# Moving the first group's casts off VectorE and reordering the start of the second group in a fused attention and routing kernel

## The chip, the cores and the metric

The kernel runs on one core of a Trainium2 chip (trn2). The metric is the device time of one execution in microseconds (us), as a median over executions. Executions of both kernels were timed in turn on the same chip, and one execution of each kernel was profiled.

Two words are used throughout. A **unit** is one head by 128 keys: TensorE (PE) makes 128x768 scores, ScalarE (ACT) takes their exp, PE multiplies with the values. **Exp n** is the exp of unit n, counted from 0; 24 units make a group (one batch, four heads), and there are eight groups. A **half-clock window** is a stretch of 3.41 us in which the granted TensorE clock, as the trace records it, is 0.50 (in the profile of the kernel before: from 43.86 to 47.28 us). In the profile lines DVE is VectorE, POOL is GpSimd and SPq is SyncE's queue.

## The reference, cut to what matters

```python
# q, k, v: (4, 8, 768, 64); proj: (64, 6)
q_bits = (q @ proj > 0); k_bits = (k @ proj > 0)      # 6 hash bits a row
mask   = bucket(q_bits)[:, :, :, None] == bucket(k_bits)[:, :, None, :]
attn   = softmax(where(mask, q @ k.T / 8, -1e9))
x      = (attn @ v) as (3072, 512)
# then: P = exp(x @ w_gate), 8 rounds of row and column scaling,
#       out = sum over 8 experts of P[:, e] * relu(x @ w1[e]) @ w2[e]
```

## The kernel before

Each group has to be prepared. VectorE turns q and k in 32x32 blocks (`turn_qk`), PE hashes them, VectorE makes bits, and the 71-row operands `ks` and `qs` of the score matmuls are put together from 64 rows of q or k and 7 rows of bits. From the second group on, GpSimd casts the turned rows to f16, transfers issued by SyncE stack the heads (`stack`), and the bits travel to DRAM and back (`put_bits`, `get_bits`). The first group does all of it with engine copies (`place`), as there is nothing else to do yet.

```python
def turn_qk(name, c):
    ...
    pin(nc.vector.transpose(o_ap, i_ap))
    if n:
        pin(nc.gpsimd.tensor_copy(t16s[name][:, c, :], trs[name][:, c, :]))

def at_once():                       # group 0
    for name in "kq":
        for c in range(2):
            turn_qk(name, c)
            place(name, 0, c, nc.scalar.copy)
            ...                      # the hash matmuls
            warm_up((0, 1, 0, 6)[2 * (name == "q") + c])
    for i, name in enumerate("kq"):
        ...                          # bits of k, then of q, on VectorE
        place_bits(name, 0)
        for c in range(2):
            if name == "k":
                place("k", 1, c, nc.scalar.copy)
                place("q", 1, c, nc.vector.tensor_copy)
    cast_v()
    for h in range(1, HG):
        for name in "kq":
            if h > 1:
                for c in range(2):
                    place(name, h, c, nc.vector.tensor_copy)
            place_bits(name, h)
...
# groups 1 to 7: at which unit of the group before each step is issued
due = (5, 6, 7, 8, 15, 17) if n == 1 else (0, lag, 2 * lag, 3 * lag, 4 + 3 * lag, 7 + 3 * lag)
...                                  # k turned, stacked
if n + 1 < len(groups):
    fetch(n + 1, "k")
...                                  # q turned, stacked, v loaded; hash, bits, put_bits
if n + 1 < len(groups):
    fetch(n + 1, "q")
...                                  # get_bits, the other heads stacked, cast_v
```

The units themselves run in a fixed order on PE, ACT and VectorE, each engine in program order. A product of two SBUF operands on VectorE, `xn`, ends each head:

```python
pin(nc.vector.tensor_tensor(xns[b][:, :, c0:c0 + D], nv[:, :, 0:D],
                            rn.unsqueeze(2).to_broadcast([P, J, D]), op=Alu.mult))
```

Near the end of attention GpSimd makes eight additions of 128x1024 f16 on the weights of expert 1 (`quarters_of_w(1)`, `quarters_of_w2(1)`).

The softmax here doesn't subtract the row's maximum and nothing guards it: scores larger than these inputs give would overflow.

Of the kernel before, what the change touches and what calls it, by code (L numbers as in the profile page):

```python
# [20 lines left out]
def kernel(  # L21
# [11 lines left out]
    nc = tc.nc  # L33
# [17 lines left out]
    HG = 4  # L51
# [10 lines left out]
    def pin(ins):  # L62
        tc.keep_in_program_order(ins)
        return ins
# [281 lines left out]
    groups = [(b, g) for b in range(B) for g in range(NGRP)]  # L346
    nat, grp = {}, {}

    def fetch(n, what, eng=nc.gpsimd):
        b, g = groups[n]  # L350
        for name, src in (("k", k), ("q", q)):
            if name in what:
                x = (12 if n else 0) + 3 * "kq".index(name)
                t = acc_flat[:, x * DD:(x + 3) * DD].rearrange("p (m d) -> p m d", d=D)
                pin(eng.dma_start(out=t, in_=src[b, g * HG:(g + 1) * HG].rearrange("h (r m) d -> (h r) m d", r=R)))
                nat[name, n] = t
        if "v" in what:
            t = lv.tile([P, HG, KT * D], F32, tag="v", name="v")
            vsrc = v[b, g * HG:(g + 1) * HG].rearrange("h (r m j) d -> m r h (j d)", r=R, m=M4)
            for m in range(M4):  # L360
                pin(eng.dma_start(out=t[R * m:R * (m + 1)], in_=vsrc[m]))
            nat["v", n] = t

    def prepare(n):
# [3 lines left out]
        trs, bts, dss, t16s = {}, {}, {}, {}  # L368
        for x, name in enumerate("kq"):
            y = (18 if n else 6) + 3 * x  # L370
            trs[name] = acc_flat[:, y * DD:(y + 3) * DD].rearrange("p (c t) -> p c t", c=2)
            d[name] = wk.tile([P, HG, S], F16, tag=name + "s", name=name + "s")
            if n == 2:
                if x == 0:
                    t16 = hpool.tile([P, FO, S], F16, tag="h", name="t16")
                t16s[name] = t16[:, 2 * x:2 * x + 2, :]
            elif n:
                t16s[name] = wk.tile([P, 2, S], F16, tag="t16", name="t16")

        def turn_qk(name, c):  # L380
            i_ap = nat[name, n][:, :, 32 * c:32 * (c + 1)]
            o_ap = trs[name][:, c, :]
            if name == "k":
                i_ap = i_ap.rearrange("p (m t) d -> p m t d", m=M4)
                o_ap = o_ap.rearrange("p (t m r) -> p m t r", t=KT, m=M4)
            else:
                o_ap = o_ap.rearrange("p (m r) -> p m r", r=R)
            pin(nc.vector.transpose(o_ap, i_ap))
            if n:
                pin(nc.gpsimd.tensor_copy(t16s[name][:, c, :], trs[name][:, c, :]))  # L390

        def stack(name, h):
            for c in range(2):
                pin(nc.sync.dma_start(out=d[name][32 * c:32 * (c + 1), h, :],
                                         in_=t16s[name][32 * h:32 * (h + 1), c, :]))
# [22 lines left out]
        def get_bits(name, h):  # L418
            pin(nc.sync.dma_start(out=d[name][D:KR, h, :].rearrange("r (j t) -> r j t", j=2),
                                       in_=dss["kq"]["kq".index(name), :, h, 0:NB + 1, :].rearrange("j r t -> r j t")))  # L420
# [6 lines left out]
        def cast_v():  # L427
            v32 = wk.tile([P, 2, 3, D], F32, tag="v32", name="v32", bufs=1)
            for i in range(2):
                hs = slice(2 * i, 2 * i + 2)  # L430
                pin(nc.gpsimd.tensor_copy(va[:, hs, :, 0:D],
                                          nat["v", n][:, hs, :].rearrange("p h (t d) -> p h t d", d=D)))
            for i in range(2):
                hs = slice(2 * i, 2 * i + 2)
                pin(nc.gpsimd.tensor_tensor(v32, va[:, hs, 0:3, 0:D], va[:, hs, 3:6, 0:D], op=Alu.add))
                pin(nc.gpsimd.tensor_tensor(v32[:, :, 0], v32[:, :, 0], v32[:, :, 1], op=Alu.add))
                pin(nc.gpsimd.tensor_tensor(vs[:, hs, 0:D], v32[:, :, 0], v32[:, :, 2], op=Alu.add))

        def place(name, h, c, copy):
            pin(copy(d[name][32 * c:32 * (c + 1), h, :], trs[name][32 * h:32 * (h + 1), c, :]))  # L440

        def place_bits(name, h):
            o, i = d[name][D:KR, h, :], d["bt"][32 * h:32 * h + NB + 1, "kq".index(name), :]
            if name == "k":
                pin(nc.vector.tensor_scalar(o, i, BIG, None, op0=Alu.mult))
            else:
                pin(nc.vector.tensor_copy(o, i))

        def at_once():
            d["bt"] = wk.tile([P, 2, S], F16, tag="t16", name="bt0")  # L450
            for name in "kq":
                pr = sps.tile([P, 2, 512], F32, tag="s", name="pr0")
                d["pr" + name] = pr
# [3 lines that stand above are left out]
                    for x in range(2):  # L457
                        pin(nc.tensor.matmul(pr[:, x, 0:HT], pb0[:, c, :], trs[name][:, c, x * HT:(x + 1) * HT],
                                             start=(c == 0), stop=(c == 1)))
                    warm_up((0, 1, 0, 6)[2 * (name == "q") + c])  # L460
            for i, name in enumerate("kq"):
                pin(nc.vector.tensor_scalar(d["bt"][:, i, :].rearrange("p (x t) -> p x t", x=2),
                                            d["pr" + name][:, :, 0:HT], 0.0, qoff[:, 0:1] if i else 0.5,
                                            op0=Alu.is_gt, op1=Alu.subtract))
                place_bits(name, 0)
                for c in range(2):
                    if name == "k":
                        place("k", 1, c, nc.scalar.copy)
                        place("q", 1, c, nc.vector.tensor_copy)
            cast_v()  # L470
            for h in range(1, HG):
                for name in "kq":
                    if h > 1:
                        for c in range(2):
                            place(name, h, c, nc.vector.tensor_copy)
                    place_bits(name, h)

        if n == 0:
            at_once()
            return  # L480

        lag = 2 if n > 2 else 1
        due = (5, 6, 7, 8, 15, 17) if n == 1 else (0, lag, 2 * lag, 3 * lag, 4 + 3 * lag, 7 + 3 * lag)
        yield due[0]
        turn_qk("k", 0)
        yield due[1]
        turn_qk("k", 1)
        stack("k", 0)
        stack("k", 1)
        if n + 1 < len(groups):  # L490
            fetch(n + 1, "k")
        yield due[2]
        turn_qk("q", 0)
# [22 lines left out]
            move_bits("q")  # L516
        put_bits()
        stack("k", 2)
        if n + 1 < len(groups):
            fetch(n + 1, "q")  # L520
        yield due[5]
        for h in range(1 if n < 3 else 0, 2):
# [6 lines left out]
        stack("q", 3)  # L529
        get_bits("k", 3)  # L530
        get_bits("q", 3)
        cast_v()

    def scores(n, h, kt):
# [104 lines left out]
    def warm_up(count):  # L639
        for _ in range(count):  # L640
            pin(nc.tensor.matmul(warm, tiny, tiny.unsqueeze(1).to_broadcast([P, 4, P]), start=True, stop=True))

    warm_up(18)
    for _ in prepare(0):
        pass
# [8 lines left out]
    due = 0  # L654
    owed = 0.0
    for u in range(len(units) + 1):
        if u < len(units):
            n, h, kt = units[u]
            b, g = groups[n]
            i = u % per  # L660
            if i == 0:
                prep = prepare(n + 1) if n + 1 < len(groups) else iter(())
                due = 0
            while due is not None and due <= i:
                due = next(prep, None)
            if n == len(groups) - 1 and i == 2:
                for _ in quarters_of_w(1):
                    pass
                for _ in quarters_of_w2(1):
                    pass  # L670
            if u + 1 < len(units):
                pts[u + 1] = scores(*units[u + 1])
# [11 lines left out]
        elif u >= 2 * per:  # L684
            owed += (total if b < 3 else total - 8 * 865) / (2 * per - 8)
            while owed > 0:
                c = next(fill, None)
# [201 lines left out]
```

## Time and profile before

| | before |
|---|---|
| median | 779.89 us (779.07 to 780.59, 3 runs) |
| profiled execution, span | 776.6 us, mean granted clock 0.996 |
| PE busy | 752.2 us, 97% |
| VectorE / ACT / GpSimd busy | 73% / 66% / 40% |
| first exp starts | 16.46 us |
| exp 33 starts | 48.83 us |

The busy shares are averages over the whole span and say that PE sets the time. The change touches the first 66 us only, so what counts is the timeline of that stretch. In a timeline each line is one instruction or several merged ones: start, length, engine, source line, operation, output and inputs with their shapes, count, and in brackets the time its engine sat idle before it with what ended that. The lines are shown in the prediction below.

### The profile page before, as it was taken

Reading aid. Unit: us, or ns where it says so; the run is one execution under the profiler, and the core shown is the slowest. Engines: PE = TensorE matmul, PEld = TensorE weight load, DVE = VectorE, ACT = ScalarE, POOL = GpSimd, SP = SyncE. Lnnn points to the kernel's source line nnn. Section 1 sums busy time; section 2 is a strip of 40 time slices with the busy share of each in tenths; the row PEclk is TensorE's granted clock in tenths of the full one; section 3 lists DMA queues with packets and bytes.
Section 4 is the critical chain, followed back from the end, with each engine's and each line's share of the span. In section 5 each row is a group of like instructions: output and inputs, shape, how many; then the busy total and the mean of one; then the engine's idle time right before and its main releaser. Section 6 shows DMA issues by size and latency. Waiting matters only on the chain.

```text
span 776.6 us, 16594 instructions
## 1 busy us (share of the span) xinstructions
PE 752.2 (97%) x6245; PEld 518.6 (67%) x6245; DVE 570.3 (73%) x1265; ACT 512.6 (66%) x1026; POOL 309.9 (40%) x313
## 2 busy tenths in 40 slices
PE   8889999999999999999999999999999999999996
PEld 3556656566554666677777777777777777777663
DVE  6867757766669677777777777777777777777774
ACT  4877776678754777766666666666666666666660
POOL 5476535357400333443344334334543344334220
PEclk9999999999999999999999999999999999999999
DMA  6679548652011464586477647754964496443334
GB/s 203 142 180 208 159 115 210 141 141 55 2 35 22 79 109 81 107 143 110 83 124 132 119 90 136 119 100 82 171 121 90 84 162 109 82 93 75 83 83 132
DMA packets 40925, 87.55 MB, mean 113 GB/s; under 512 B 7028, under 2 KB 21196, under 8 KB 40844
## 3 DMA queue, kind: packets, MB, share of 16 engines
q0 software_dynamic: 27152, 69.49, 46.7%
q1 hardware_dynamic: 13020, 16.21, 8.0%
q8 instruction: 49, 0.80, 0.4%
q10 hardware_dynamic: 672, 0.79, 0.4%
q14 instruction: 32, 0.26, 0.1%
HBM read 53.01 MB, written 6.98 MB: 77 GB/s over the span
## 4 chain that ended last, share of the span: by engine, by line
PE 82%; DVE 7%; ACT 6%; DMA 2%; issue 2%; SPq 0%; ACTq 0%; DVEq 0%
PE a L767 18%; PE a L245 17%; PE d L767 13%; PE y L245 9%; PE st L538 5%; PE d L245 4%; PE hp L600 4%; ACT pt L541 4%; PE yp L610 3%; PE num L554 3%; PE hp L318 1%; PE pr L400 1%; PE yp L302 1%; ACT acc L236 1%; DVE hT L776 1%
## 5 line engine op out<-in xcount | busy, mean ns | idle before, releaser
L776 DVE CUSTOM_DVE_ANT_0 hT<-d,u 128x384 f16<-128x384 f32 x336 | 185.7, 553 | 96.0 <-ACT u L772 95.2
L249 ACT ACTIVATE vt<-a,p 128x256 f32<-128x256 f32 x324 | 153.2, 473 | 149.2 <-PE a L245 148.8
L541 ACT ACTIVATE pt<-st 128x768 f16<-128x768 f32 x192 | 146.5, 809 | 49.3 <-PE st L538 48.8
L772 ACT COPY u<-a 128x384 f32<-128x384 f32 x336 | 160.8, 479 | 23.0 <-PE a L767 20.6
L284 POOL DMA_DIRECT2D acc<-vt x72 | 61.3, 852 | 267.6 <-ACT vt L249 114.1
L245 PEld LDWEIGHTS <-hT 128*128 128x128 f16 x1296 | 126.3, 97 | 50.8 <-DVE hT L776 1.1
L245 PE MATMUL a<-t,hs 128*128 128x256 f16 x972 | 145.8, 273 | 2.1 <-ACT vt L249 1.0
L245 PEld LDWEIGHTS <-hs 128*128 128x128 f16 x972 | 94.8, 98 | 38.5 <-issue 2.8
L767 PEld LDWEIGHTS <-t 128*128 128x128 f16 x896 | 87.7, 98 | 36.1 <-issue 0.3
L767 PE MATMUL a<-xT,s 128*128 128x384 f16 x448 | 109.4, 326 | 0.2
L767 PE MATMUL d<-xd,t 128*128 128x384 f16 x448 | 109.4, 326 | 0.0
L538 PE MATMUL st<-qs,ks 71*128 71x384 f16 x384 | 94.2, 327 | 7.1 <-ACT pt L541 2.7
L245 PE MATMUL y<-t,hT 128*128 128x256 f16 x648 | 97.1, 272 | 0.0
L253 DVE SCALAR_TENSOR_TENSOR acc<-y,p,acc 128x256 f32<-128x256 f32 x162 | 77.5, 479 | 11.4 <-PE y L245 11.4
L554 PEld LDWEIGHTS <-pt 128*128 128x128 f16 x1152 | 60.8, 98 | 27.4 <-issue 1.4
L767 PEld LDWEIGHTS <-s 128*128 128x128 f16 x672 | 65.5, 98 | 17.5 <-issue 2.6
L554 PE MATMUL num<-va,pt 128*128 128x65 f16 x1152 | 66.8, 194 | 1.3 <-DVE nv L565 0.7
L806 ACT ACTIVATE hT<-a 128x384 f16<-128x384 f32 x112 | 54.0, 483 | 1.8 <-PE a L767 1.7
L767 PE MATMUL a<-xd,s 128*128 128x384 f16 x224 | 54.3, 323 | 0.8 <-ACT u L772 0.6
L767 PE MATMUL d<-xT,t 128*128 128x384 f16 x224 | 54.7, 326 | 0.0
L767 PE MATMUL a<-xT,t 128*128 128x384 f16 x224 | 54.7, 326 | 0.0
L538 PEld LDWEIGHTS <-ks 71*128 71x128 f16 x384 | 33.5, 98 | 31.5 <-issue 16.2
(116 smaller groups left out, 987.4 us busy)
## 6 DMA issues: line engine op xcount, KB each, us to landing
acc<-vt POOLq DMA_DIRECT2D x72, 512.0 KB, 4.8
t<-in_moe_w_dram POOLq DMA_DIRECT2D x24, 512.0 KB, 7.7
v<-in_v_dram POOLq DMA_DIRECT2D x28, 192.0 KB, 6.0
out_dram<-acc SPq DMA_DIRECT2D x82, 64.0 KB
acc<-in_k_dram POOLq DMA_DIRECT2D x6, 768.0 KB, 5.9
acc<-in_q_dram POOLq DMA_DIRECT2D x6, 768.0 KB, 13.2
t<-in_moe_w_dram POOLq DMA_DIRECT2D x4, 1024.0 KB, 12.4
ks<-t SPq DMA_DIRECT2D x56, 48.0 KB
```

What stands on the lines that cost most here:

```text
L245: pin(nc.tensor.matmul(dst, hq[hn][:, fo, :], wq[wn][:, fo, :], start=first and fo == 0, stop=fo == FH - 1, skip_group_check=True))
L249: pin(nc.scalar.activation(out=vt[:, k], in_=a, func=Act.Copy, scale=p))
L253: pin(nc.vector.scalar_tensor_tensor(out=dst, in0=src, scalar=p, in1=dst, op0=Alu.mult, op1=Alu.add))
L284: pin(nc.gpsimd.dma_start(out=acc[:, b, i], in_=vt, accum_op=Alu.add))
L538: pin(nc.tensor.matmul(st[:, i, 0:HT], d["k"][0:KR, h, kt * P:(kt + 1) * P], d["q"][0:KR, h, i * HT:(i + 1) * HT], start=True, stop=True))
L541: pin(nc.scalar.activation(out=pt, in_=st[:, :, 0:HT], func=Act.Exp, scale=scale))
L554: pin(nc.tensor.matmul(num[:, j * (D + 1):(j + 1) * (D + 1)], pf[:, j * P:(j + 1) * P], va[:, h, kt, :], start=(kt == 0 and j == 0), stop= ...
L600: pin(nc.tensor.matmul(hp[:, 0:HT], w1[:, do, fo * P:(fo + 1) * P], xT[:, do, b * S + t * HT:b * S + (t + 1) * HT], start=(do == 0), stop= ...
L767: pin(nc.tensor.matmul(bk, wq[wn][:, do, f * P:(f + 1) * P], xq[xn][:, do, :], start=first and do == 0, stop=do == 1, skip_group_check=True))
L772: pin(nc.scalar.copy(t, bk))
L776: pin(add(TENSOR_ADD_SAT, out=dst, in0=bk, in1=u, s0=3e38, s1=0.0))
L806: pin(nc.scalar.activation(out=hT[:, f, hi], in_=a, func=Act.Relu))
```

## The change

Its intent is to relieve VectorE in the opening, and to get the bits of the second group on their way sooner. The first group's late heads (k heads 2 and 3, q heads 1 to 3) are cast by GpSimd in whole tiles and stacked by ten SyncE transfers. The second group is turned at units 3 to 6 and hashed at 9, and the third group's loads move behind its bits in program order.

```diff
-            if n == 2:
+            if n in (0, 2):
                 ...                  # room for the f16 copies of group 0
-            if n:
-                pin(nc.gpsimd.tensor_copy(t16s[name][:, c, :], trs[name][:, c, :]))
+            pin(nc.gpsimd.tensor_copy(t16s[name][:, c, :], trs[name][:, c, :]))
...
-                    warm_up((0, 1, 0, 6)[2 * (name == "q") + c])
+                    warm_up(6 if name == "q" and c else 0)
+                for h in range(2 if name == "k" else 1, HG):
+                    stack(name, h)
...
-                for c in range(2):
-                    if name == "k":
-                        place("k", 1, c, nc.scalar.copy)
-                        place("q", 1, c, nc.vector.tensor_copy)
+            for c in range(2):
+                place("k", 1, c, nc.scalar.copy)
             cast_v()
             for h in range(1, HG):
                 for name in "kq":
-                    if h > 1:
-                        for c in range(2):
-                            place(name, h, c, nc.vector.tensor_copy)
                     place_bits(name, h)
...
-        due = (5, 6, 7, 8, 15, 17) if n == 1 else (...)
+        due = (3, 4, 5, 6, 9, 12) if n == 1 else (...)
...
-        if n + 1 < len(groups):      # twice: for k and for q
+        if n > 1 and n + 1 < len(groups):
...
+        if n == 1:
+            fetch(2, "kq")           # after get_bits
         cast_v()
```

More of the change, by code (lines that the diff above doesn't have):

```diff
@@ L376, in prepare @@
                 t16s[name] = t16[:, 2 * x:2 * x + 2, :]
-            elif n:
+            else:
                 t16s[name] = wk.tile([P, 2, S], F16, tag="t16", name="t16")
@@ L482, in prepare @@
         lag = 2 if n > 2 else 1
-        due = (5, 6, 7, 8, 15, 17) if n == 1 else (0, lag, 2 * lag, 3 * lag, 4 + 3 * lag, 7 + 3 * lag)
+        due = (3, 4, 5, 6, 9, 12) if n == 1 else (0, lag, 2 * lag, 3 * lag, 4 + 3 * lag, 7 + 3 * lag)
         yield due[0]
@@ L518, in prepare @@
         stack("k", 2)
-        if n + 1 < len(groups):
+        if n > 1 and n + 1 < len(groups):
             fetch(n + 1, "q")
```

## The prediction

> **What bounds the kernel now.** I read the page first (engine shares, slices, chain), then the windows of the first 66 us, then the timelines of PE, ACT, DVE, GpSimd and of the SyncE queue over the same stretch, and last the chain of waits from 6 to 50 us. The page and the windows:
>
> ```profile
> PE 752.2 (97%) x6245; PEld 518.6 (67%) x6245; DVE 570.3 (73%) x1265; ACT 512.6 (66%) x1026; POOL 309.9 (40%) x313
> ...
> PE 82%; DVE 7%; ACT 6%; DMA 2%; issue 2%; SPq 0%; ACTq 0%; DVEq 0%
> ...
> 42.00:50.00 8.00, 6.46 (x59) 3.08 (x60) 5.60 (x11) 4.04 (x6) 7.84 (x13) 0.79 0.56 170
> 50.00:66.00 16.00, 14.65 (x205) 10.32 (x203) 10.30 (x21) 15.85 (x23) 9.22 (x15) 1.00 0.88 206
> ```
>
> The whole kernel hangs on TensorE. The shares of DVE, ACT and DMA in the chain lie mostly in the first 66 us, where the first of eight groups (a batch and four of its heads; a group is 24 units, one head by 128 keys each) get going: group 0 must be turned, hashed and scored before anything else exists to do. The change touches only this opening. In the good stretch (50 to 66) ACT is busy 15.85 of 16 us: there the exp of each unit is the limit. From 42 to 50 ACT is busy only half the time and the mean granted clock is 0.79: something is lost there. The exps of line 541 show what (start, length, engine, idle before, releaser):
>
> ```profile
> 23.65 3.69 ACT L541 ACTIVATE pt<-st 128x768 f16<-128x768 f32 x5
> 27.91 0.81 ACT L541 ACTIVATE pt<-st 128x768 f16<-128x768 f32 x1 [0.57 <-PE st L538]
> 30.22 0.81 ACT L541 ACTIVATE pt<-st 128x768 f16<-128x768 f32 x1 [1.50 <-PE st L538]
> 32.83 1.51 ACT L541 ACTIVATE pt<-st 128x768 f16<-128x768 f32 x2 [1.80 <-PE st L538]
> ...
> 43.86 1.59 ACT L541 ACTIVATE pt<-st 128x768 f16<-128x768 f32 x2 [1.39 <-PE st L538]
> 47.38 0.81 ACT L541 ACTIVATE pt<-st 128x768 f16<-128x768 f32 x1 [1.93 <-PE st L538]
> 48.83 1.51 ACT L541 ACTIVATE pt<-st 128x768 f16<-128x768 f32 x2 [0.64 <-PE st L538]
> ```
>
> The reader is to see two holes, 27 to 33 and 42 to 49 us. The steady pace is the first fifteen exps in 10.88 us, 0.725 us a unit. The first exp starts at 16.46, so unit 17 should start at 16.46 + 17 x 0.725 = 28.79; it starts at 32.83: **4.04 us lost**. Exps 0 to 29 are done at 42.4, so exp 33 should start three paces later, at 44.6; counting two exps from 43.86 and one at 47.38, it is the one at 48.83: **4.2 us lost**. What they wait for is in the chain:
>
> ```profile
> 28.72 0.94 DVE acc L388
> ...
> 30.36 0.60 DVE xn L570
> 30.97 0.05 issue
> 31.01 0.51 PE xp L576 x6
> 31.52 0.83 PE pr L400 x8
> ...
> 34.26 6.99 DMA ds<-bt
> ...
> 41.60 1.54 DMA qs<-ds
> ```
>
> In the first hole VectorE is late: its queue still holds group 0's casts when group 1's transposes, the division of the heads and the turn of x come due. In the second, the bits of group 1 travel to DRAM in 6.99 us and back in 1.54 us, behind 768 KB of v and 768 KB of the third group's q; PE stands 1.53 us before the scores of unit 30. Right after it the window 43.9 to 47.2 shows a granted clock of 0.50, for one stretch of about 3.4 us, the only one after the start.
>
> [...] one window at 0.50 follows a window (40.4 to 43.8) in which PE was busy 1.87 of 3.40 us. [...] the placing of k bits (7x768 f16) takes 0.35 us while GpSimd rests and 0.86 us at 15.87 us, when GpSimd holds a 0.92 us addition; the f32 transposes take 0.90 to 0.98 us with or without GpSimd. [...] SyncE's loads, which land in the order of their issue, the last (q of group 1) at 17.0 us.
>
> **The change, part by part.**
>
> (1) Start. VectorE now does this between k's bits and the first score:
>
> ```profile
> 12.66 0.35 DVE L445 TENSOR_SCALAR ks<-bt 7x768 f16<-7x768 f16 x1
> 13.04 1.11 DVE L440 CAST qs<-acc 32x768 f16<-32x768 f32 x2
> 14.19 1.02 DVE L462 TENSOR_SCALAR bt<-pr,qoff 128x768 f16<-128x768 f32 x1
> 15.24 0.60 DVE L447 COPY qs<-bt 7x768 f16<-7x768 f16 x1
> ```
>
> The two casts in between (1.11 us) go. The q bits then wait for the q hash, which ends on PE at 10.88 + 2.83 = 13.71, not for the casts at 14.15. So they start about 0.45 us sooner, and their placing at about 14.75 meets the end of GpSimd's first v cast (14.03 to 14.83) rather than the middle of the second: 0 to 0.25 us more[...]. First score at about 15.4 instead of 15.94: **0.5 us saved**. The single warm-up matmul that goes sat beside this wait, worth nothing.
>
> (2) Late heads. Ten casts of 32x768 go from VectorE: the pair of part (1), 1.11 us, and four more pairs in its timeline up to 24 us, 1.80 + 1.26 + 1.12 + 1.12 us. Together 6.41 us leave VectorE before 24.3. In their place GpSimd makes four 128x768 casts (0.83 us each, 3.3 us, at 8 to 12.6 us, where it idled 8.55 us for v), and SyncE issues ten transfers of 48 KB at 0.57 us each, from about 8.8 to 15.6. These are off the path if they land in time. They queue behind group 1's loads, which end at 17.0; 480 KB at the 220 GB/s that the 1536-byte v rows showed is 2.2 us, so the last lands near 19.3 and the third pair (q head 1) near 18.3. Unit 6 wants q head 1 at 15.4 + 6 x 0.725 = 19.8. It fits by about 1.5 us.
>
> (3) First hole. With VectorE free some 6 us sooner (its bits placed at about 18 to 19.5 us instead of 24.3), group 1's four transposes (3.8 us) run at units 3 to 6 and are done by about 23, in time for the hash at units 9 and 10 (22.4 to 23.8). The hash itself stays: sixteen matmuls are one 1.43 us piece in every later group. So is a turn of x, which the second stretch shows at about 0.15 us net. Lost then: 1.43 + 0.15, call it 1.6 with the split, instead of 4.04: **2.4 us saved**. The hash no longer falls on the unit of the turn of x.
>
> (4) Second hole. The bits of group 1 leave at about 25 instead of 34.3 us. Even with another 7 us on the way and 2 us back they are there at 34; unit 30 comes at 15.9 + 30 x 0.725 + 1.6 = 39.3. The 1.53 us wait goes, and with PE no longer idle so does the half-clock window. Lost then: only group 2's hash, about 1.4 us, instead of 4.2: **2.8 us saved**.
>
> (5) Third group's loads. They leave GpSimd after v of group 1 and the gate weights, near 26 to 27 us; before, k left at 27.0 and q at 33.5. They land by about 33, and group 2 is turned from unit 24, near 35. Nothing on the path. Nothing else in the program changes.
>
> Sum: 0.5 + 2.4 + 2.8 = 5.7 us. From 66 us on PE is busy 131.5 of 134 us and then 563 of 576, with waits that move along with it, so the gain should go through to the end. I take off 0.5 us for a short wait at unit 9 or 10, where the transposes end close to the hash. 779.9 - 5.2 = **774.7 us**.
>
> **The rivals.** A: the stacked heads come late. Ten small transfers sit behind 1.5 MB on the same queue. For it: the margin at unit 6 is estimated, and the DMA engines are full until 17 us, as the DMA view of 0 to 24 us shows (40 slices of 0.6 us):
>
> ```profile
> DMA  0000192899999999999999899992000000000000
> ```
>
> Against it: this queue goes empty at 17 us and stays so until 26. A wait of 2 us plus a half-clock window would eat about 3 us and leave 777.5. B: GpSimd becomes the bound of the opening, as it also converts v (14.0 to 20.0 us) and now starts group 1's casts right behind. [...] Against it: those casts are needed only by unit 24. Worst, part (3) gives 1 us less: 775.7. C: the bits' round trip still ends late, since all of the third group's 1.5 MB now meets it instead of half: the 7 us could become some 13, an estimate from the same rate. Then unit 30 waits as before and only (1) and (3) remain: 777. Against it: nine microseconds of lead. D: the half-clock window comes back elsewhere[...]; about 1.5 us: 776.2. E: all goes a little better, as no wait is left at the hash and the exps close ranks: 773.5.
>
> **Range and chances.** The parts are worth 5.2, and A, B, C, D each take at most 3 us and are not all likely at once; the runs of the kernel before lie within 1.5 us. So 772.8 to 777.6 holds it 8 times in 10. 2% is 15.6 us, more than all the idle time in the opening could give: faster 0.005, within 0.985, slower 0.01 (only a new long wait or more half-clock windows would do that).
>
> **What would show it.** First exp at about 16.0 instead of 16.46. No casts of 32x768 on VectorE at 13 to 24 us. Exp 17 at about 29.9 instead of 32.8 and exp 33 near 43 (15.97 + 33 x 0.725 + 3.0) instead of 48.8. No wait for a bits transfer in the PE timeline at 40 to 44 us and the granted clock 1.00 throughout. Wrong would be a PE wait on a transfer into ks or qs near 19 to 21 us, or a clock of 0.50 in the opening, or a gain in the first 66 us that the span doesn't show.

The 0 to 0.25 us in part (1) is an estimate, the 0.60 us of placing q's bits beside a GpSimd cast of v less the 0.35 us of k's bits without one. That the half-clock window goes with the wait (part 4) was an estimate from the one window of this trace, and so was its 1.5 us in rival D. The transposes took 0.93 to 0.98 us. The last of each of SyncE's loads landed at 6.93 (k), 9.80 (q), 10.63 to 13.88 (four of v), 15.41 and 17.27 us (k and q of group 1).

## The result

| | before | after |
|---|---|---|
| median | 779.48 us (779.01 to 780.59, 4 runs) | 774.41 us (773.42 to 776.04, 4 runs) |
| ratio | | 0.9935, 95% interval 0.9912 to 0.9958 |
| profiled execution, span | 776.6 us | 771.7 us |

A ratio is the mean time of one kernel's fast runs over that of the other's of the same rounds, so it is not quite the ratio of the medians. The time came out at 774.4 us against 774.7 predicted: faster, by less than 2%.

Now the profile after. On its page the chain that ended last gives DVE and DMA a smaller share and ACT a larger one; the windows view (stretch; busy time of PE, PEld, DVE, ACT and GpSimd with counts; granted clock; DMA share; GB/s) shows the full clock where 0.79 stood:

```profile
PE 83%; ACT 8%; DVE 6%; issue 2%; DMA 1%; SPq 0%; ACTq 0%; DVEq 0%
...
42.00:50.00 8.00, 7.32 (x98) 5.09 (x95) 4.30 (x11) 7.38 (x12) 2.12 (x4) 1.00 1.06 233
```

The exps of the profile after, in the timeline of ACT:

```profile
15.09 7.29 ACT L539 ACTIVATE pt<-st 128x768 f16<-128x768 f32 x10 [1.52 <-PE st L536]
22.97 0.81 ACT L539 ACTIVATE pt<-st 128x768 f16<-128x768 f32 x1 [0.59 <-PE st L536]
24.37 4.40 ACT L539 ACTIVATE pt<-st 128x768 f16<-128x768 f32 x6 [0.59 <-PE st L536]
29.33 11.02 ACT L539 ACTIVATE pt<-st 128x768 f16<-128x768 f32 x15 [0.57 <-PE st L536]
41.27 0.81 ACT L539 ACTIVATE pt<-st 128x768 f16<-128x768 f32 x1 [0.92 <-PE st L536]
42.67 16.90 ACT L539 ACTIVATE pt<-st 128x768 f16<-128x768 f32 x23 [0.59 <-PE st L536]
```

Counting 10 + 1 + 6 exps puts exp 17 at 29.33, and 15 + 1 more put exp 33 at 42.67. Both holes are gone but for short gaps of 0.57 to 0.92 us: two at a hash of group 1, one at the turn of x, two at a hash of group 2. VectorE's timeline after, between k's bits and the first score, has no casts:

```profile
11.94 0.35 DVE L444 TENSOR_SCALAR ks<-bt 7x768 f16<-7x768 f16 x1
13.02 1.02 DVE L463 TENSOR_SCALAR bt<-pr,qoff 128x768 f16<-128x768 f32 x1 [0.73 <-PE pr L457]
14.08 0.39 DVE L446 COPY qs<-bt 7x768 f16<-7x768 f16 x1
```

q's bits wait for their hash (0.73 us), as foreseen. And SyncE's queue shows the bits of group 1 leaving at 25.77 and the transfer back issued at 30.28 (it waits for their arrival in DRAM). In the chain before they arrived at 34.26 + 6.99 = 41.25, so this is 11.0 us sooner:

```profile
25.77 0.53 SPq L415 DMA_DIRECT2D ds<-bt  x1
...
30.28 0.30 SPq L418 DMA_DIRECT2D ks<-ds  x1
```

**Where the gain goes later.** I laid the 1026 ACT instructions of the two profiles side by side and took the lead of the new kernel at each. It is 1.37 us at exp 0, 3.50 at exp 17, 6.16 at exp 33, then constant at 6.2 to 6.4 until 186 us (times of before); between 186 and 200 us it falls to 4.53, and it is 4.49 at the last ACT instruction. So 1.8 us that the opening had won are lost in one place, where GpSimd adds up the weights of expert 1. VectorE's products `xn` of that stage, and the PE wait that follows from one, in the timelines before, with the first addition beside the first product:

```profile
184.21 0.56 DVE L570 TENSOR_TENSOR xn<-nv,rn 128x384 f16<-128x384 f32 x1
184.27 2.48 POOL L139 TENSOR_TENSOR s<-t 128x1024 f16<-128x1024 f16 x1
...
189.88 1.57 DVE L570 TENSOR_TENSOR xn<-nv,rn 128x384 f16<-128x384 f32 x1
```

and after:

```profile
177.61 2.12 POOL L139 TENSOR_TENSOR s<-t 128x1024 f16<-128x1024 f16 x1
177.85 2.29 DVE L568 TENSOR_TENSOR xn<-nv,rn 128x384 f16<-128x384 f32 x1
...
180.66 0.81 PE L598 MATMUL hp<-xT,t 128*128 128x384 f16 x4 [0.84 <-DVE hT L601]
...
184.52 2.29 DVE L568 TENSOR_TENSOR xn<-nv,rn 128x384 f16<-128x384 f32 x1
```

An `xn` of 0.56 us takes 2.29 us when it starts 0.24 us after a GpSimd addition of 2.12 us has begun; the relu behind it on VectorE is late, the tile of matmul results that it reads isn't free, and PE waits 0.84 us. After the change PE waits so for 0.84, 0.84 and 0.66 us, before it once for 0.55: this is the 1.8 us. A product that starts late waits the addition out: in the two profiles the five that start inside one (at 189.88 and 196.09 us before; 177.85, 184.52 and 191.45 after) end 0.41 or 0.42 us after it. Where the product started first, 0.06 us ahead, it took 0.56 us and the addition 2.48. Which products are hit is a matter of phase between two engines that nothing ties together there. In the ten profiles with uncut additions (the experiments below, without the slow execution) the first `xn` of the stage decides: where it starts 0.01 to 0.06 us before the first addition, it takes 0.56 us and the loss stays away (three profiles); where it starts 0.02 to 0.31 us after it, it takes 2.22 to 2.51 us and the loss comes (seven).

### The profile page after: what moved, and what is told of

It is laid out like the page before. It is cut to its first block, busy times and chain, and to the rows that moved or that the text cites. A ratio compares the mean times of both kernels' runs of the same rounds, so it can differ in the third digit from the quotient of the medians.

```text
span 771.7 us, 16609 instructions
## 1 busy us (share of the span) xinstructions
PE 748.7 (97%) x6244; PEld 518.0 (67%) x6244; DVE 565.0 (73%) x1255; ACT 512.4 (66%) x1026; POOL 313.3 (41%) x317
## 4 chain that ended last, share of the span: by engine, by line
PE 83%; ACT 8%; DVE 6%; issue 2%; DMA 1%; SPq 0%; ACTq 0%; DVEq 0%
PE a L765 18%; PE a L245 18%; PE d L765 13%; PE y L245 9%; ACT pt L539 5%; PE st L536 5%; PE d L245 4%; PE hp L598 4%; PE yp L608 3%; PE num L552 3%; PE hp L318 1%; PE pr L399 1%; PE yp L302 1%; ACT acc L236 1%; DVE hT L774 1%
```

## The experiments

"Before" in a line is the kernel before, timed in the same rounds.

### The changed kernel again

No edit; the question is what varies from run to run.

> The changed kernel once more, to see what varies from run to run. Theory: the gain in the opening is fixed (exp 33 at about 42.7 to 43.5 us instead of 48.8 before), the rest varies by two things: half-clock windows (a mean clock under 0.997 goes with a longer span) and the phase of GpSimd's additions on the first weights against VectorE's xn products near 175 to 195 us (0.56 us each when free, up to 2.3 us[...]). Expected ratio 0.9935 give or take 0.002. Rival: the varying 1.3 us is noise spread over the whole kernel; then the lead over the kernel before, exp by exp, would drift slowly instead of stepping.

Measured: 774.63 us median (773.63 to 778.47, 6 runs), before 780.62 us (778.1 to 783.36, 11 runs), ratio 0.9929 (0.9906 to 0.9951). The execution that was profiled took 776.61 us, and its windows of 3.41 us around the first scores show why:

```profile
14.41:17.82 3.41, 2.05 (x17) 1.10 (x17) 3.35 (x5) 1.94 (x3) 3.17 (x5) 1.00 1.01 301
17.82:21.23 3.41, 3.41 (x32) 2.32 (x31) 3.36 (x6) 2.89 (x5) 1.93 (x5) 0.50 0.21 51
```

PE is busy 2.05 of 3.41 us in the first window, and the clock is 0.50 in the next and the two after it, until 28.06. The lead over the first profile of before falls from 0.58 us at exp 0 to -4.39 at exp 13, by 4.97 us; in the first profile of the changed kernel it falls by 1.35 there, as its hash comes at unit 9 and the old one only at 15. So the windows cost 3.6 us. In the first profile of the changed kernel the window that starts at 14.86 had PE busy 2.70 us, and none followed. The program is the same. The window took in two short PE waits, 0.75 us before the first scores and 0.57 us for the first exp. The first of them was 0.29 us in the first profile, where VectorE placed q's bits in 0.39 us; here that took 0.85 us, beside a GpSimd cast of v (14.22 to 15.05 us):

```profile
14.40 0.85 DVE L446 COPY qs<-bt 7x768 f16<-7x768 f16 x1
15.36 0.81 PE L536 MATMUL st<-qs,ks 71*128 71x384 f16 x4 [0.75 <-issue]
```

With the waits of the first profile no stretch of 3.41 us around the first scores, wherever it begins, has PE busy less than 2.49 us. So the length of the first wait matters; what the place of the 3.41 us grid does was not tried by itself. The four runs at mean clocks of 0.998 and 0.999 took 773.6 to 774.9 us, those at 0.991 and 0.992 took 778.5 and 776.6. The expectation was half right: the loss steps, it doesn't drift, but the opening's gain is not fixed at all.

### The first group's part alone

```diff
-        due = (3, 4, 5, 6, 9, 12) if n == 1 else (...)
+        due = (5, 6, 7, 8, 15, 17) if n == 1 else (...)
-        if n > 1 and n + 1 < len(groups):     # both places; fetch(2, "kq") removed
+        if n + 1 < len(groups):
```

> Only the first group's part: casts on GpSimd and stacking by transfer, while group 1 keeps its old units (5 to 8, hashed at 15) and the third group's loads their old places. Theory: the start (0.5 us) and the first hole (about 2.1 us) come from this part alone, since it is VectorE's casts that made group 1 late. The bits leave near 31 instead of 34.3 us and return near 40, and unit 30 comes near 38.6, so a wait of about 1 us stays, perhaps with a half-clock window: gain 3 to 4.5 us of the 5, ratio 0.994 to 0.996. Rival: the gain is all in the units and the loads of group 1; then the ratio is above 0.998.

Measured: 777.91 us (774.82 to 779.16, 6 runs), ratio 0.9957 (0.9936 to 0.9978). In the profile the lead at exp 33 is 6.14 us, as large as with the whole change: both holes go with this part alone. The bits leave at 30.55 and are back in time. But a wait turns up 24 units later, as PE waits before unit 54 for the bits of group 2, and a half-clock window follows at 60.99:

```profile
58.88 0.48 PE L534 MATMUL st<-qs,ks 71*128 71x384 f16 x2 [1.31 <-DMA qs<-ds]
```

That takes the lead from 6.07 to 3.36 us. My wait was expected at unit 30; it came at unit 54. The size of the gain was as expected.

### The second group's part alone

```diff
 # the kernel before, with
-        due = (5, 6, 7, 8, 15, 17) if n == 1 else (...)
+        due = (3, 4, 5, 6, 9, 12) if n == 1 else (...)
 # and the third group's loads after get_bits, as in the change
```

> Only the second group's part: group 1 turned at units 3 to 6, hashed at 9, third group's loads behind its bits, while VectorE keeps the ten casts of group 0. Theory: this part alone cannot gain in the first hole: the transposes still stand behind the casts, which end at 24.3 us, so the hash at unit 9 (near 23 us) waits until about 28 us, some 4 us and perhaps a half-clock window; the second hole goes (2.7 us). Net ratio 0.998 to 1.003. Rival: the parts are independent and add up; then it gains about 2.7 us, ratio 0.9965.

Measured: 780.0 us (778.95 to 786.62, 4 runs), ratio 1.0007 (0.9972 to 1.0041), as expected. The hash of group 1 comes due at 22.4 us, but the transposes stand behind the casts on VectorE:

```profile
24.75 0.84 PE L400 MATMUL pr<-acc,pb 128*32 128x384 f32 x4 [2.32 <-DVE acc L388]
26.47 1.50 PE L400 MATMUL pr<-acc,pb 128*32 128x384 f32 x4 [0.88 <-DVE acc L388]
```

Two half-clock windows follow (25.7 to 32.5 us). The lead is -7.2 us at exp 13; it is back at -0.38 at exp 33, as the second hole is gone. The parts don't add up: the second is worth nothing without the first.

### The changed kernel with group 1 at its old units

```diff
-        due = (3, 4, 5, 6, 9, 12) if n == 1 else (...)
+        due = (5, 6, 7, 8, 15, 17) if n == 1 else (...)
```

> The changed kernel with group 1 back at units 5 to 8 and hashed at 15, but the third group's loads still after its bits in program order. It tells whether the second hole went because the bits leave early or because the loads no longer meet them. Theory (bits early): they leave near 30.5 us, GpSimd issues the loads near 27.5 to 28.5 us whatever their place in the program, so the round trip still meets them, 5 to 8 us; a wait of 0 to 1 us before unit 30 comes back; ratio 0.9935 to 0.996. Rival (loads behind the bits is what counts): no wait before unit 30 and the round trip is 3 us; ratio as the changed kernel, 0.9935.

Measured: 777.47 us (776.13 to 779.14, 6 runs), ratio 0.9956 (0.9938 to 0.9975). The bits leave at 30.15 and need 6.70 us to DRAM although the loads stand behind them in the program: GpSimd issued those at 28.03, as it waits for nothing there. PE stands before unit 30 and again before unit 48, where it waits for stacked q rows of group 2:

```profile
39.66 0.48 PE L536 MATMUL st<-qs,ks 71*128 71x384 f16 x2 [1.72 <-ACT pt L539]
...
55.40 0.48 PE L536 MATMUL st<-qs,ks 71*128 71x384 f16 x2 [1.08 <-DMA qs<-t]
```

The view names ACT as the releaser of the first, but its exp was long done; the bits of q were issued at 37.21 and are what arrived last (inferred). So it is the early leaving of the bits that keeps unit 30 from waiting, not the place of the loads behind them; the wait was longer than the 0 to 1 us that I expected.

### The changed kernel with the third group's loads in their old places

```diff
-        if n > 1 and n + 1 < len(groups):     # both places
+        if n + 1 < len(groups):
-        if n == 1:
-            fetch(2, "kq")
```

> The changed kernel with the third group's k loaded right after group 1's k is stacked, and its q right after the bits leave, as in the kernel before. Theory: the loads' place is not what removes the second hole in the changed kernel, as its bits came back at 30.3 us and unit 30 comes at about 38 us; the k load goes out some 4 us earlier and delays group 1's v by about 2 us, which has slack. Ratio 0.9935 give or take 0.002, no wait on a bits transfer before unit 30. Rival: with the loads ahead of the bits the wait comes back; ratio 0.9965 and a wait of over 0.5 us at unit 30 or at unit 54.

Measured: 775.78 us median of 6 runs, ratio 0.9941 (0.9918 to 0.9963). The profiled execution took 2721 us and counts as slow: its 128x384 f16 matmuls took about 900 ns instead of 326 and, back to back, started 630 ns apart instead of 162, which is about a quarter of the pace. Its trace holds no record of the clock at all, so the 1.00 listed for it says nothing, and I found no cause in it. It says nothing about the change and is left out. The five others took 772.48 to 776.32 us.

> The changed kernel with the third group's loads in their old places, again for its profile, as the first profiled execution fell in a state in which all matmuls took several times as long (2721 us). Theory: no wait on a bits transfer before unit 30 and at most a short one at unit 54; exp 33 at 42.7 to 43.5 us where no half-clock window falls in the opening. Rival: a wait of over 0.5 us at unit 30.

Measured: 777.93 us, one run, state unknown. Exp 33 starts at 42.77 and there is no wait before unit 30, as expected. But PE waits before unit 54, and two half-clock windows follow:

```profile
59.41 0.80 PE L534 MATMUL st<-qs,ks 71*128 71x384 f16 x2 [1.91 <-DMA qs<-ds]
```

The third group's k, loaded earlier, goes ahead of group 1's v, whose conversion on GpSimd begins at 32.80 instead of 29.99 us; the bits of group 2 leave at 45.21 instead of 43.73 and arrive in DRAM at 54.46 instead of 51.56. So the place of the loads does matter, though for group 2's bits and not for group 1's. It probably does so in some executions only, as the median of the timed runs is within the noise of the changed kernel's; no other execution was profiled. My theory was wrong there.

### The kernel before again

No edit.

> The kernel before once more, for a second profile of it. Theory: first exp near 16.0 to 16.5 us (the loads of q land between 9.1 and 9.8 us in all profiles so far, whatever the kernel), a hole of 4 us with exps 15 to 17 and one of 4 us, or more with half-clock windows, at exps 30 to 33 with PE waiting for a bits transfer, exp 33 at 48 to 52 us. Rival: the two holes were a matter of that one execution.

Measured: 780.56 us, one run, state unknown. Both holes are there: exp 17 starts at 32.11, exp 33 at 48.30, and PE waits 1.80 us for the bits before unit 30, with one half-clock window after it at 43.04. PE also waits 1.06 us before unit 54, for stacked q rows, so a wait at that place does not need half of the change to arise. The first exp starts at 16.25 although q landed 0.76 us sooner than in the first profile. In this execution the stage of the additions also went the bad way: against the first profile of before it loses 1.8 us there. So that loss is not the change's doing. Of the ten profiles with uncut additions, leaving out the slow one, it falls in seven (before again, after, first part, second part, old loads again, no warm-ups, more warm-ups) and not in three (before, after again, old units).

### Without the warm-up matmuls before the first scores

```diff
-                    warm_up(6 if name == "q" and c else 0)
+                    warm_up(0 if name == "q" and c else 0)
```

> The changed kernel without the six warm-up matmuls that stand between the q hash (ends near 12.8 to 13.3 us) and the first scores (14.6 to 15.4 us). It should make TensorE idle about 2 us there, so that a 3.4 us window around it has PE busy under about 2.1 us. Theory (what PE does in a window decides about half-clock windows, and those explain most of the spread of the runs): one to three half-clock windows follow near 15 to 28 us in most runs; median 2 to 5 us longer than the changed kernel, 777 to 779 us, mean clock 0.990 to 0.994. Rival (the windows come at random): same median as the changed kernel, 774 to 775 us.

Measured: 777.51 us (775.06 to 778.11, 6 runs), ratio 0.9963 (0.9941 to 0.9985); mean clock 0.991 to 0.993 in all six.

```profile
13.28:16.68 3.40, 1.37 (x12) 0.84 (x13) 3.30 (x6) 1.52 (x4) 3.17 (x6) 1.00 1.03 354
16.69:20.10 3.41, 3.38 (x30) 2.09 (x27) 3.37 (x5) 2.85 (x5) 1.96 (x4) 0.50 0.30 67
```

Taking away six matmuls that compute nothing costs time: 777.5 us against the 774.4 and 774.6 us of the changed kernel. By the ratios to the kernel before (0.9963 against 0.9935 and 0.9929, with intervals that overlap a little) it is 2.2 to 2.7 us. In the profile PE is busy 1.37 us in the window, three half-clock windows follow, and the lead falls from 1.20 us at exp 0 to -3.65 at exp 13, 3.5 us more than the 1.35 of the changed kernel's first profile. The half-clock windows do not come at random.

### More warm-up matmuls

```diff
-                    warm_up(6 if name == "q" and c else 0)
+                    warm_up(8 if name == "q" and c else 0)
...
+            if u == 1:
+                warm_up(2)
             if u + 1 < len(units):
                 pts[u + 1] = scores(*units[u + 1])
```

> The changed kernel with eight instead of six warm-up matmuls before the first scores and two more in the 0.57 us in which PE waits for the first exp (each 0.215 us). Theory: the window around the first scores then always has PE busy over 2.4 us, and the half-clock windows at 17 to 28 us go; median 773 to 774 us instead of 774.5, mean clock 0.997 to 0.999 in nearly all runs and fewer runs above 776 us. Rival: no change, or 0.4 us more because the first scores wait for the warm-ups.

Measured: 773.91 us (773.34 to 774.39, 6 runs), ratio 0.9927 (0.991 to 0.9944); mean clock 0.997 to 0.999 in all six. The spread shrinks to 1.05 us from the 4.84 us of the changed kernel. The median moves by 0.5 to 0.7 us against the changed kernel's, which is a comparison across chips and within the noise: the ratios are 0.9927 against 0.9935 and 0.9929.

### Halved additions

```diff
-        pin(nc.gpsimd.tensor_tensor(s[:, 0], a21, a22, op=Alu.add))
+        add_on_pool(s[:, 0], a21, a22, Alu.add, cut)   # cut = 2: two halves; the same for all eight
```

> The changed kernel with each of GpSimd's eight additions on expert 1's weights (128x1024, 2.1 us) near 178 to 196 us cut into two of 128x512. Theory: a VectorE product of two SBUF operands (xn, 0.56 us free) waits out the GpSimd addition[...], so it takes at most about 0.56 + 1.1 us instead of 2.3; the stage then loses 0 to 0.6 us instead of 0.0 to 1.8: median about 1 us shorter than the changed kernel, and xn under 1.7 us in the profile. Rival: VectorE doesn't get in between the halves and xn stays at over 2 us; or the loss is elsewhere and nothing moves.

Measured: 772.03 us (771.5 to 772.23, 5 runs), ratio 0.9902 (0.9884 to 0.992). The four `xn` of the stage take 1.24 to 1.50 us; so VectorE gets in between two halves that follow each other without a gap (the first `xn` ends at 180.29 us, inside the two halves of 178.73 to 181.31). And the lead over the first profile of before doesn't fall there but grows, from 5.29 to 5.99 us: that profile too had lost something. The gain over the changed kernel is by the ratios some 2 us, more than the 1 us expected. No half-clock window is in its opening.

### Both, and the additions in four

The edits of the last two experiments together; in the second kernel the additions are cut in four along their last axis.

> The changed kernel with the four more warm-up matmuls and the halved additions together. If the two losses (half-clock windows near the first scores[...]) are separate, the gains add: median 771.5 to 772.5 us with a spread under 1 us, at or a little under the halves alone (772.0); rival: the halves alone had no half-clock windows in any run, so the warm-ups add nothing or cost up to 0.4 us.

> As the run before it, with the additions cut into four of 0.55 us each along their last axis. Theory: xn waits at most 0.6 us more, so under 1.2 us, and PE no longer waits in the stage near 178 to 196 us: another 0 to 0.5 us, median 771 to 772. Rival: the cut costs GpSimd more than it saves (32 instructions more of overhead), median as the halves or above.

The two losses meant are the half-clock windows near the first scores and the long `xn`.

Measured: both, 770.83 us (770.59 to 772.76, 6 runs), before 779.67 us (777.92 to 783.03, 11 runs), ratio 0.9888 (0.9868 to 0.9908); in four, 770.89 us (770.54 to 772.13, 5 runs), ratio 0.9882 (0.9863 to 0.9902). One `xn` of the stage in each:

```profile
183.13 1.50 DVE L578 TENSOR_TENSOR xn<-nv,rn 128x384 f16<-128x384 f32 x1
```

```profile
183.52 0.69 DVE L578 TENSOR_TENSOR xn<-nv,rn 128x384 f16<-128x384 f32 x1
```

Halves are enough: the shorter products (0.65 to 1.02 us in four, 1.24 to 1.50 in halves) gain nothing more. Both kernels give the reference's result and beat the changed kernel and the one before: 770.8 against 774.4 and about 779.7 us, ratios 0.9888 and 0.9882 against 0.9935. The spread under 1 us that I expected did not come: two of the six runs took 772.3 and 772.8 us at mean clocks of 0.997 and 0.995. What the warm-ups add to the halves alone (ratio 0.9902) stays open, as the intervals overlap.

### What the windows have in common

The windows view, laid on the grid of the recorded clock changes (before: 6.32, 43.86 and 47.28 us, whole steps of 3.41 apart), gives PE's busy time in each 3.41 us window of the opening for the thirteen profiles. The window just ahead of a half-clock stretch had PE busy 1.88 (before), 1.61 (before again), 2.05 (after again), 1.87 (first part), 1.00 (second part), 2.23 (old units), 1.38 (no warm-ups) and 1.59 us (old loads again). No window at full clock with more than 2.23 us was followed by one. Between 2.09 and 2.22 us three were not (before again, first part, halves), so near that value the busy time alone doesn't tell. The steady pace of units keeps PE at 2.7 to 3.3 us (after, 14.86 to 59.24 us). So in this stretch PE waits of about a microsecond in all (1.3 us in after again) can cost their own length and then the window.

## Why the prediction was right

| step of the prediction | predicted | measured (first profiles of each) |
|---|---|---|
| start to exp 0 | 0.5 us | 16.46 to 15.09: 1.37, of which 0.72 is q landing sooner (transpose of q at 9.11 instead of 9.83) |
| first hole, exp 0 to 17 | 2.4 us | 16.37 to 14.24: 2.13 |
| second hole, exp 17 to 33 | 2.8 us | 16.00 to 13.34: 2.66 |
| short wait at unit 9 or 10 | -0.5 us | none |
| rest of the span | 0 | -1.8 at GpSimd's additions, +0.4 in the last microseconds |

**Start.** Right. q's bits waited for the hash and not for casts, and their placing took 0.39 us instead of 0.60. The landing of q is no effect of the change, as the kernel before had it 0.76 us sooner in its second profile. Counted from the turn of q, which leaves the landing out, the first exp comes 5.98 to 6.45 us later with the first part (ten profiles, mean 6.21) and 6.62 to 7.18 without it (three, mean 6.81): 0.6 us, near the 0.5. Over these ten the placing of q's bits takes 0.35 to 0.85 us, more than the 0 to 0.25 us that the prediction allowed for a GpSimd instruction beside it.

**Late heads.** Right: no profile with the first part shows a PE wait for a stacked row at units 6 to 23, so rival A did not come. SyncE's ten issues ended at 18.56 us and not at 15.6 as estimated, but q head 1, which unit 6 takes at 18.80, was issued before the other q heads, at 11.90 and 12.57.

**First hole.** Right in cause, 0.3 us too large. The hash ran at 21.59 us on the first halves of q and k, which were turned by then, and at 22.99 on the second, turned by 21.99: no wait arose. The turn of x cost more than I allowed: exp 17 waits 0.57 us there, since the product `xn` of that head was still late by 0.36 us. The second-part experiment shows the cause: with VectorE's casts left in, PE waits 3.2 us for the same hash.

**Second hole.** Right in cause and size. The bits came back long before unit 30. But what I put under rival C, that the bits' way is long, is nearer than I thought: the way took 4.5 us with the whole change, 6.70 with the old units and over 9 us for group 2 with the old loads. With half of the change a wait stood before unit 48 or 54, and in the second profile of the kernel before there was one before unit 54 too. I had looked at the deadline of group 1 only.

**The half-clock window.** I took it as a consequence of the one wait. That was an estimate from one window: in the 3.40 us ahead of it PE was still busy for 1.87. I gave 1.5 us to its coming back elsewhere (rival D). This was the part most undersized: one execution of the changed kernel had three such windows at the first scores and lost 3.6 us to them; one run of that kernel took 778.47 us, outside the range that I gave for the median. The expectation that the granted clock would be 1.00 throughout held for the first profile of the changed kernel and not for the second.

**The rest of the span.** I said that a gain in the first 66 us that the span doesn't show would be wrong. That happened, 1.8 us of it, in the stage of GpSimd's additions. The claim that all waits there move along with the gain was the failing step: the phase of GpSimd against VectorE is set by when a load of v lands (it landed at 171.77 us after and 178.44 before, its conversion began at 171.92 and 178.59; with the lead of 6.30 taken off that is 172.29, so 0.37 us earlier against ACT's instructions), and the phase decides. The second profile of before had the same loss, so it is a draw that both kernels take part in, and the medians contain some of it on either side. So the closeness of 774.4 to 774.7 is in part luck: the landing of q (+0.7) and the missing wait (+0.5) against the additions (-1.8).

What stays open: why the clock comes back after one window in some profiles and after two or three in others while PE is busy throughout (3.42 us of the one window at 43.86 in before; 3.42, 3.41 and 3.41 us of the three at 17.82 to 28.06 in after again; 3.38 to 3.42 us of the three at 16.69 to 26.93 without the warm-ups), and what made the one execution of 2721 us slow.

## What to carry to other kernels

Each of these was seen in this kernel only. A step that stands behind a busy engine's other work in program order can't be moved forward until that engine is relieved: the second half of this change was worth nothing alone (ratio 1.0007). When a wait for a round trip is taken away, check the same deadline of the next round too, as a wait may stand there (1.31 us before unit 54 with the first part alone); and in a stretch where PE is only just busy, fill short PE waits with matmuls that compute nothing, since the half clock after them can cost more than the waits (3.6 us after 1.3 us of waits in one execution; with four more such matmuls the spread of the runs was 1.05 us instead of 4.84). Where long GpSimd instructions run beside VectorE's products of two SBUF operands, try cutting them: halves lengthened the stretch of additions by 1.1 us (19.08 against 17.97), shortened the longest `xn` of the stage from 2.29 to 1.50 us, and the loss of 1.8 us did not come.
